# Convolution, Gelu and two matmuls on one core: a new order for the first transfers, diagonals on GpSimd, and taps in two calls

## The chip, the cores and the metric

The kernel runs on one core of a Trainium2 chip. The metric is device time in microseconds (us) per execution. A run of a one-core program has no second core to compare with, so its state is taken from the time alone; every run told here counted as fast. Each run also has a mean granted TensorE clock, 1.0 being full speed.

Two terms recur. The *software ring* is the DMA queue whose transfers GpSimd issues; SyncE and ScalarE issue to hardware queues (q0 software_dynamic, q1 and q10 hardware_dynamic on the page). *Slot* means one piece of work of TensorE and ScalarE: twelve first-layer matmuls and one Gelu of 1.02 us behind them. Blocks 0 to 5 have eight slots each.

## The reference

```python
def attn(x, weight):                      # x: [8, 4096, 192], weight: [8 heads, 7]
    w = softmax(weight, axis=-1)
    # causal, depthwise: each head's 7 weights serve its 24 channels
    return sum(w[h, k] * x_pad[:, s + k, h*24:(h+1)*24] for k in range(7))

def moe(x, w_in, w_out):                  # x: [32768, 192], w_in: [192, 2048], w_out: [2048, 192]
    h = x @ w_in
    g = 0.5 * h * (1.0 + erf(h / sqrt(2)))
    return g @ w_out

out = moe(attn(x, weight).reshape(32768, 192), w_in, w_out)
```

(Written shorter than the original, with the same arithmetic. All inputs and outputs are float32.)

## The kernel before

Blocks of 256 tokens (six of them), then of 512, from two halves of the token range at once. Blocks 0 and 1 are convolved on TensorE with diagonal matrices `dg` made of the tap weights, all later ones on VectorE, tap by tap (ScalarE makes the first tap of three of them). TensorE multiplies by `W_in`, ScalarE applies Gelu, and TensorE multiplies the previous block's result by `W_out` between the slots of the current one. The parts that matter here are all about the start:

```python
# GpSimd: W_in in three parts (256, 256 and 512 columns of each half), cast to bf16 by the DMA
win_in(FP[0], FP[1], S_WIN[0])
...                                        # two affine selects make the identity
for i in range(1, 3):
    win_in(FP[i], FP[i + 1], S_WIN[i])
halo(0); halo(1)                           # cut: block 0 needs shifted copies between rows
for p in range(NP):
    cast(g, 1, p)                          # x of block 1 to bf16
for i in range(4):                         # W_out to bf16, a quarter at a time
    g.wait_ge(S_WOUT[i], 16)
    o = 2 * WG[i] * C
    g.tensor_copy(wout[:, o : o + 4 * C], woutf[:, o : o + 4 * C]).then_inc(S_WOG)

# SyncE: all other loads
load(sp, 0, (0, 1))                        # half of block 0's x; ScalarE issues the other half
sp.wait_ge(S_WIN[0], 32)                   # first part of W_in has landed
load(sp, 1)
for i in range(4):
    sp.dma_start(woutf[...], woutt[...]).then_inc(S_WOUT[i], 16)
load(sp, 2)
load(sp, 3)

# VectorE: one tap of the convolution, three calls (p = 0, 1, 2), blocks 2 and later
ins = v.scalar_tensor_tensor(dst, src, wk, a, op0=ALU.mult, op1=ALU.add)

# TensorE, while block 1's slots run: the second layer of block 0
if n == 1 and un in ((0, 0, 0), (0, 0, 4)):
    t.wait_ge(S_WOG, 2 + un[2] // 2)
```

## Time and profile before

| | before |
|---|---|
| time, median of 4 runs | 682.74 us (682.60 to 683.16) |
| span of the profiled run | 680.6 us |
| mean granted clock | 1.0 |
| first Gelu | 10.10 us |
| first matmul of block 1 | 18.34 us |
| first Gelu of block 2 | 29.73 us |
| x of block 0, of block 1, of block 2 landed | 5.91, 12.75, 19.2 us |
| W_in parts landed | 6.67, 8.69, 10.69 us |
| W_out quarters landed | 13.60, 14.65, 15.71, 17.40 us |

(682.81 us was the median of the three runs known at the time of the prediction.) From 18.34 us on, TensorE works without a gap, so from there only what would hold TensorE up can cost time. Ahead of that, everything waits for data, and all of the weights, plus x of the first three blocks, come through the same sixteen DMA engines in the first 20 us, whose share is 1.13 from 4 to 15 us and 1.25 from 15 to 20 (the windows are below). The prediction shows the lines.

### The profile page before, as it was taken

How to read it: one execution, taken by the hardware profiler on the slowest of the kernel's cores; microseconds unless marked ns; L12 is line 12 of the kernel's file. 1: busy time of each engine (PE TensorE's matmuls, PEld its weight loads, DVE VectorE, ACT ScalarE, POOL GpSimd, SP SyncE). 2: the span in 40 equal slices, each digit the busy share in tenths (PEclk: the TensorE clock that was granted, in tenths of full speed). 3: DMA queues.
4: the chain of work that ended last, by engine and by line, in shares of the span. 5: the costliest groups of instructions: out<-in, count | busy, mean ns of one | idle time of the engine just before them, and what ended most of it. 6: DMA issues, size and time to landing. Idle time of an engine off the chain costs nothing.

```text
span 680.6 us, 27316 instructions
## 1 busy us (share of the span) xinstructions
PE 674.6 (99%) x12576; PEld 407.5 (60%) x12576; DVE 561.7 (83%) x906; ACT 536.5 (79%) x548; POOL 38.9 (6%) x57
## 2 busy tenths in 40 slices
PE   8999999999999999999999999999999999999998
PEld 4999655555555555555555555555555555555557
DVE  6999989888889888899888898888898888988611
ACT  6899987787787877787777788777778777778772
POOL 5126000000000000000000000000000000000000
PEclk9999999999999999999999999999999999999999
DMA  9446233134442133331244422334322444310123
GB/s 223 88 99 138 64 71 81 43 69 95 96 94 61 45 87 94 95 89 46 59 95 94 94 70 45 78 94 96 89 56 47 95 94 96 80 40 25 48 50 94
DMA packets 132994, 54.79 MB, mean 81 GB/s; under 512 B 126480, under 2 KB 132752, under 8 KB 132880
## 3 DMA queue, kind: packets, MB, share of 16 engines
q1 hardware_dynamic: 130960, 51.50, 32.6%
q8 instruction: 98, 1.61, 1.0%
q0 software_dynamic: 1248, 0.79, 0.9%
q10 hardware_dynamic: 672, 0.76, 0.4%
q14 instruction: 16, 0.13, 0.1%
HBM read 28.66 MB, written 25.17 MB: 79 GB/s over the span
## 4 chain that ended last, share of the span: by engine, by line
PE 98%; ACT 1%; DMA 1%; DVE 0%; SPq 0%; issue 0%; ACTq 0%
PE hp L763 48%; PE ob L823 43%; PE ob L793 5%; PE hp L793 1%; DMA xin<-in_x_dram 1%; ACT gT L684 1%; PE ob L714 0%; ACT xc L191 0%; DVE xT L529 0%; ACT xTb L633 0%; SPq L871 0%; DVE osb L283 0%; SPq L332 0%; ACTq L632 0%
## 5 line engine op out<-in xcount | busy, mean ns | idle before, releaser
L684 ACT ACTIVATE gT<-hp 128x1024 bf16<-128x1024 f32 x512 | 523.2, 1024 | 129.0 <-PE hp L763 125.7
L763 PE MATMUL hp<-xc,win 64*64 64x512 bf16 (+2 forms) x6048 | 418.6, 366 | 1.5 <-ACT gT L684 1.1
L823 PE MATMUL ob<-gT,wout 64*64 64x512 bf16 x5376 | 366.3, 376 | 0.0
L562 DVE SCALAR_TENSOR_TENSOR acc<-xT,wcol,acc 128x512 f32<-128x512 f32 (+1 forms) x495 | 314.5, 699 | 0.0
L763 PEld LDWEIGHTS hp<-xc,win 64*64 64x64 bf16 (+1 forms) x6048 | 187.6, 106 | 136.1 <-ACT gT L684 2.6
L823 PEld LDWEIGHTS ob<-gT,wout 64*64 64x64 bf16 x5376 | 172.1, 118 | 123.0
L314 DVE STREAM_TRANSPOSE osb<-ob 128x512 f32<-128x512 f32 x84 | 74.1, 885 | 99.9 <-PE ob L823 99.9
L529 DVE STREAM_TRANSPOSE xT<-xin 128x512 f32<-128x512 f32 (+1 forms) x105 | 78.5, 797 | 3.4 <-DMA xin<-in_x_dram 3.4
L562 DVE SCALAR_TENSOR_TENSOR xc<-xT,wcol,acc 128x512 bf16<-128x512 f32 (+1 forms) x99 | 65.1, 712 | 0.0
L450 POOL COPY xT<-xT 128x18 f32<-128x18 f32 x30 | 27.9, 929 | 505.3 <-DVE xT L529 483.0
L793 PE MATMUL ob<-wout,gT 64*128 64x192 bf16 x896 | 46.8, 243 | 0.0
L793 PEld LDWEIGHTS ob<-wout,gT 64*128 64x128 bf16 x896 | 38.6, 94 | 5.2 <-issue 0.4
L555 DVE TENSOR_SCALAR acc<-xT,wcol 128x512 f32<-128x512 f32 (+1 forms) x90 | 37.5, 473 | 1.1
L698 PE MATMUL hp<-warm 128*128 128x512 bf16 x16 | 5.5, 516 | 1.3 <-DVE warm L466 1.3
L285 ACT ACTIVATE osb<-ob 128x192 f32<-128x192 f32 x2 | 0.7, 331 | 7.1 <-PE ob L793 7.1
L793 PE MATMUL hp<-wout,gT 64*128 64x192 bf16 x128 | 5.9, 243 | 0.0
L283 DVE COPY osb<-ob 128x192 f32<-128x192 f32 x2 | 0.7, 358 | 6.1 <-PE ob L793 6.1
L793 PEld LDWEIGHTS hp<-wout,gT 64*128 64x128 bf16 x128 | 5.3, 94 | 0.0
L657 ACT ACTIVATE acc<-xT,wcol 128x256 f32<-128x256 f32 (+1 forms) x9 | 5.2, 575 | 0.0
L270 ACT ACTIVATE osb<-ob 128x384 f32<-128x384 f32 x10 | 4.9, 486 | 0.0
L698 PEld LDWEIGHTS hp<-warm 128*128 128x128 bf16 x16 | 1.9, 126 | 4.3 <-issue 2.5
L387 POOL DMA_DIRECT2D win<-in_moe_w_in_dram x6 | 3.9, 660 | 0.8 <-POOLq L904 0.8
(36 smaller groups left out, 31.4 us busy)
## 6 DMA issues: line engine op xcount, KB each, us to landing
out_dram<-osb SPq DMA_DIRECT2D x122, 192.0 KB, 3.1
xin<-in_x_dram SPq DMA_DIRECT2D x116, 192.0 KB, 4.1
xin<-in_x_dram SPq DMA_DIRECT2D x20, 96.0 KB, 4.3
woutf<-in_moe_w_out_dram SPq DMA_DIRECT2D x4, 384.0 KB, 5.9
win<-in_moe_w_in_dram POOLq DMA_DIRECT2D x4, 96.0 KB, 4.6
win<-in_moe_w_in_dram POOLq DMA_DIRECT2D x2, 192.0 KB, 5.1
out_dram<-osb SPq DMA_DIRECT2D x8, 48.0 KB, 1.7
out_dram<-osb ACTq DMA_DIRECT2D x4, 96.0 KB, 2.0
```

The lines of the kernel that those rows point to most:

```text
L270: e.activation(out=dst, in_=src, func=AF.Copy).then_inc(S_EVA)
L314: v.transpose(ap(osb[m % 2], j, [[8 * C, 128], [C // 2, TB // 32], [NP, 32]]), bank(ring(m, j)),).then_inc(S_EV)
L450: g.tensor_copy(dst, src).then_inc(S_HALO)
L529: v.transpose(ap(xT[n % 2], p * XW + HX, [[NP * XW, 128], [1, w]]), ap(xin[n % NX], p, [[TB // 32 * DQ, 128], [D if n == 0 else DQ, w // 3 ...
L555: ins = v.tensor_scalar(a, src, wk, None, ALU.mult)
L562: ins = v.scalar_tensor_tensor(dst, src, wk, a, op0=ALU.mult, op1=ALU.add)
L657: a.activation(out=acc[n % 2][:, p * TB : p * TB + w], in_=ap(xT[n % 2], p * XW + HX, [[NP * XW, 128], [1, w]]), func=AF.Copy, scale=wcol[ ...
L684: a.activation(out=ap(gT[n % 2], i * c * 2 * w, dst), in_=ap(hp[u % 2], 0, src), func=AF.Gelu,).then_inc(S_GELU)
L698: t.matmul(hp[1][:, 0:512], warm[:, 0:128], warm[:, :])
L763: ins = t.matmul(hp[u % 2][fo : fo + fw, o : o + w], ap(win, f1, [[NP * F, 64], [2, fw]]), xc[n % 2][r, p * TB : p * TB + w], start=(p == ...
L793: ins = t.matmul(bb[sub], gT[m % 2][r, c0 : c0 + 128], wout[r, CH[sub][i] * C : (CH[sub][i] + 1) * C], start=(ph == 0 and i == 0), stop=(p ...
L823: ins = t.matmul(bank(ring(m, j), slice(64 * h, 64 * h + 64), w), ap(wout, 64 * hf * NF * C + CH[h][i] * C + j, [[NF * C, 64], [NP, 64]],) ...
```

## The change

Its intent: start block 0 and block 1 sooner. The software ring carries half of W_in, then x of block 1, then the other half; so x of block 1 arrives earlier than on SyncE behind W_in. GpSimd makes `dg`, which frees VectorE of 0.63 us (the trace before). x of block 0 comes in half rows of 96 floats and needs no shifted copies. VectorE does a tap in two calls (two thirds, then one), and the three transposes of a block in one.

```diff
 # GpSimd
-            win_in(FP[0], FP[1], S_WIN[0])
             g.wait_ge(S_MSET, 1)
             ...                                   # affine selects
-            for i in range(1, 3):
-                win_in(FP[i], FP[i + 1], S_WIN[i])
+            win_in(FP[0], FP[1], [S_WIN[0]] * 2)
+            load(g, 1, (0, 2), S_XP)
+            g.wait_ge(S_PRO, 9)
+            g.wait_ge(S_IDN, 2)
+            g.tensor_tensor(dg, idb, wcol, ALU.mult).then_inc(S_DG)      # shortened
+            load(g, 1, (1, 3), S_XP)
+            win_in(FP[1], FP[2], S_WIN[1:])
 # SyncE
-            sp.wait_ge(S_WIN[0], 32)
-            load(sp, 1)
-            for i in range(4):
-                sp.dma_start(woutf[...], woutt[...]).then_inc(S_WOUT[i], 16)
-            load(sp, 2)
+            sp.wait_ge(S_WIN[1], 16)
+            for k in range(3):
+                wout_in(k)
+            load(sp, 2)
+            wout_in(3)
             load(sp, 3)
 # SyncE and ScalarE, loads of block 0: as all others now
-                if n == 0:
-                    dst = [[TB // 32 * DQ, 32], [1, mb * D - DQ]]
-                    src = [[mb * D, 32], [1, mb * D - DQ]]
-                else:
-                    dst = ...
+                dst = [[TB // 32 * DQ, 32], [DQ, mb], [1, DQ]]
+                src = [[D, 32], [32 * D, mb], [1, DQ]]
 # VectorE
-            def conv(n, k, p):                     # p in 0, 1, 2
+            def conv(n, k, s):                     # s in 0, 1
+                p0, pn = (0, 2) if s == 0 else (2, 1)
 # TensorE
-            for i in range(16):                    # warm-up
+            for i in range(10):
-            share = {1: [4, 12, 8, 8, 8, 8, 8, 8]}
+            share = {1: [4, 4, 4, 10, 10, 10, 11, 11]}
-                        if n == 1 and un in ((0, 0, 0), (0, 0, 4)):
-                            t.wait_ge(S_WOG, 2 + un[2] // 2)
+                        if n == 1 and un[:2] == (0, 0) and un[2] % 4 == 0:
+                            t.wait_ge(S_WOG, 1 + un[2] // 4)
```

Cut: the order of W_out's chunks to match, the semaphores' counts, the order of TensorE's convolutions and of its first slot, block 0's copies out of the convolution, and the store of block 0. `share` says how many pieces of block 0's second layer TensorE does behind each slot of block 1.

## The prediction

> **What bounds the kernel now.** I read the page first, parts 1, 2 and 4.
>
> ```profile
> PE 674.6 (99%) x12576; PEld 407.5 (60%) x12576; DVE 561.7 (83%) x906; ACT 536.5 (79%) x548; POOL 38.9 (6%) x57
> PE   8999999999999999999999999999999999999998
> PE 98%; ACT 1%; DMA 1%; DVE 0%; SPq 0%; issue 0%; ACTq 0%
> ```
>
> TensorE is busy in 99% of the span, only the first and last slices are below nine tenths, and the chain that ended last is 98% TensorE. So whatever the change does to VectorE over the long middle is hidden, and it can move only the start, some 20 us. I then read the chain in order of time over the first 32 us.
>
> ```profile
> 1.64 4.26 DMA xin<-in_x_dram
> ...
> 7.02 0.97 PE ob L714 x18
> ...
> 9.12 0.28 ACT xc L191
> ...
> 9.45 0.63 PE hp L763 x8
> 10.08 0.02 issue
> 10.10 1.94 ACT gT L684 x2
> 12.04 0.01 issue
> 12.05 1.03 ACT gT L684
> 13.09 0.05 issue
> 13.13 0.83 PE hp L763 x12
> ...
> 17.26 1.03 ACT gT L684
> 18.29 0.04 issue
> 18.34 0.83 PE hp L763 x12
> ```
>
> The chain is: x of block 0 lands at 5.90, is transposed and cast, goes through the convolution on TensorE (L714), is copied out by ScalarE, then meets W_in (L763) and the first Gelu at 10.10. Block 0 has eight slots, each with a Gelu of 1.02 us against 0.66 us of matmul, so ScalarE paces it. Block 1 starts at 18.34, and from there TensorE never waits. What ScalarE lost in between is in the timeline of the start.
>
> ```profile
> 12.77 1.34 DVE L529 STREAM_TRANSPOSE xT<-xin 128x256 f32<-128x256 f32 x3 [1.93 <-DMA xin<-in_x_dram]
> 13.36 1.47 POOL L213 CAST xTb<-xT 128x256 bf16<-128x256 f32 x3 [5.53 <-DVE xT L529]
> 15.98 1.02 ACT L684 ACTIVATE gT<-hp 128x1024 bf16<-128x1024 f32 x1 [0.95 <-PE hp L763]
> 17.26 3.96 ACT L684 ACTIVATE gT<-hp 128x1024 bf16<-128x1024 f32 x4 [0.25 <-PE hp L763]
> 19.24 1.35 DVE L529 STREAM_TRANSPOSE xT<-xin 128x256 f32<-128x256 f32 x3 [0.77 <-DMA xin<-in_x_dram]
> ```
>
> x of block 1 lands only at 12.77; its cast comes late, TensorE stands in front of block 1's convolution, and ScalarE waits 0.95 + 0.25 = 1.20 us. The last line matters for the rivals: x of block 2 lands at 19.24, and VectorE's taps hang on it.
>
> [...]
> - [...] 15 taps of 256 columns take 6.02 us (0.40 each), 15 of 512 take 10.04 us (0.67 each). So a tap is about 0.13 us plus 1.05 ns per column. [...]
> - [...] For the 448 columns of the diagonals [...] VectorE takes 0.63 us here. No line of this trace shows such an operation on GpSimd.
> - [...] New x of block 0 is in rows of 384 B. The part of the page on queues over the first 24 us gives 42 ns per packet on the hardware queue of SP (61.3% of 16 x 24 us, over 5552 packets) and 360 ns per packet of 5760 B on ACT's queue (6.0%, over the 64 data packets).
> - [...] the warm-up's weight loads follow 0.43 us apart until 5.05, and then six take 1.18 us. The new kernel has 10 warm-up matmuls, not 16.
>
> **The change part by part.**
> 1. *x of block 0 in half rows.* Old: four loads of 180 KB, each row read twice; 128 packets x 360 ns / 16 engines = 2.9 us of the engines. New: four of 96 KB in 384-byte rows; 1024 packets x 42 ns / 16 = 2.7 us, at the 27 ns that the whole run's average gives (32.6% of the span over 130960 packets) 1.7 us. W_in's first half is issued after the two affine selects, about 0.5 us later than its first quarter was, so it crowds x less. I choose a landing 0.5 us sooner, at 5.4 (between 0 and 0.9). The shifted copies on GpSimd (three of 0.39 us) go, but they ran beside ScalarE's casts and ended with them (7.68 against 7.72), so that alone is worth nothing.
> 2. *Diagonals on GpSimd.* The tap weights are there at 4.6 as before. GpSimd has by then issued two parts of W_in and two of x, four issues of 0.65 us from about 1.9, until 4.6. [...] The convolution can start at 5.4 + 0.05 + 0.54 + 0.47 = 6.5, where it was 7.02. [...]
> 3. *Copying out of block 0.* ScalarE had four copies (0.38, 0.38, 0.28, 0.28) and now has three, VectorE has the fifth piece. The last one moves forward by 0.30 us. The first slot now does both chunks' first two thirds before it needs the last third: four matmuls (0.27 us) remain after that copy instead of eight (0.63). I count 0.45 us of the possible 0.6, since the first eight matmuls must also be done.
> 4. *First Gelu:* 10.10 - 0.5 - 0.45 = 9.15.
> 5. *The duplication of W_in* is now in halves: two copies of 0.98 us from 8.5 to 10.5, and the third slot needs them; it could start at 10.15. Its matmul of 0.66 to 0.83 us then ends 0.1 to 0.25 after the second Gelu: a loss of 0.15.
> 6. *x of block 1 on the software ring*, issued at about 3.3 to 4.6 and 5.7 to 7.0, lands near 9.5 by the ring's 4.6 us from issue. Transposes run from 10.5, GpSimd's casts of 0.49 each end near 12.5, in time for its convolution behind slots 3 to 5. So the 1.20 us of ScalarE's waits go.
> 7. *Second half of W_in*, issued at 7.1 to 8.4, lands at 12 to 13; slot 4 wants it at 12.3. A loss of 0 to 0.5 us; I count 0.2.
> 8. *W_out* is issued only when that has landed, at about 12.1 where it was 8.5. Landed at 15 to 17, cast in pieces of 0.88 us. The first second-layer matmuls come near 17.1 and take four units in each of the first three slots, in the order in which the pieces land. I count 0.1 us there, with nearly no slack.
> 9. *Taps in two calls.* In a block of 256 a tap of three calls is 3 x 0.40 = 1.20 us; now 0.67 + 0.40 = 1.07. Over six such taps 0.8, the first tap (0.29 per 256, 0.41 per 512 columns) 0.18 and the joined transposes 0.2 make 1.1 us per block. In blocks of 512: 0.13 x 6 + 0.1 + 0.2, about 1.1 us in each of the 29, which takes some 33 us from VectorE's 561.7 (to near 529). None of it is on the path in the middle, but it is needed in blocks 2 and 3: there the taps ended at 28.62 and 39.17, while TensorE started these blocks at about 28.79 and 39.3. An earlier TensorE without faster taps would have run into VectorE.
>
> Sum: 0.5 + 0.45 + 1.20 - 0.15 - 0.2 - 0.1 = 1.7 us at the start of block 1. Block 1's first three slots become paced by ScalarE (1.03 against 0.99 us of TensorE work), another 0.1; I leave 0.2 more for what block 2 may cost. So 1.4 us of 682.81: 681.4 us.
>
> **The rivals.**
> - *The wait moves to x of block 2.* Its loads are behind three parts of W_out that wait for W_in. If they land at 19.7 rather than before 19, the taps (1.15 + 0.70 + 6 x 1.07 = 8.27 us) end at 28.0, and block 2 cannot start much before 27.6, where 27.3 is wanted. For it: DMA is saturated until 20 now. Against: 336 KB less is moved, and VectorE's chain is shorter by 1.1 us. The gain would be 0.9 to 1.1 us: 681.8.
> - *GpSimd becomes the bound of the start.* If its issues or the diagonals take half as long again, [...] all that follows on its ring shifts by 1 us: W_in's second half lands at 13.5, and ScalarE waits a microsecond at slot 4. Against: the six issues were steady at 0.62 to 0.78 us. Gain about 0.3: 682.5.
> - *A cold TensorE.* The warm-up now ends near 5.3 and leaves a gap before 6.5. [...] the convolution (1.69 us) and the first slots run up to twice as long: 1 to 2 us lost, 683. Against: in the trace the clock was full from 5.05.
> - *All goes well* and x lands at 5.0, nothing stalls: 2.1 us gained, 680.7.
>
> **Range and chances.** The whole start up to 18.34 holds only some 9 us of waits and ramp, most of it the fixed chain of landing, transpose, convolution, Gelu; 2% would be 13.7 us. A gain beyond 2% would need the middle to move, and TensorE has no gap there; a loss beyond 2% would need VectorE to fall behind by a third of a microsecond in each block, and it becomes faster. So within 2% is nearly certain. The four cases give 680.7 to 683; I take 680.6 to 682.6 around 681.4.
>
> **What would show it.** Right: the first transpose at about 5.4; the first Gelu near 9.2; no ScalarE wait of 0.9 us between slots 5 and 6; block 1's first matmul near 16.6; VectorE busy near 529 us with TensorE's busy time unchanged but for the warm-up; no wait of TensorE for VectorE at block 2. Wrong: a tensor_tensor line of GpSimd well over 1.2 us, or ending after 6.5; a transposition of block 2 that waits for DMA past 19.5; W_in waits in front of slot 4; matmuls of 0.43 us after 6 us; or waits of TensorE past 40 us, which would mean that the taps or evacuations in the middle were on the path after all.

## The result, and the profile after

The changed kernel took 686.78 us (median of 4 runs, 686.50 to 687.35). The ratio to before is 1.0058, 95% interval 1.0043 to 1.0072. Ratios here and below are the mean time of one kernel's fast runs over that of the other's of the same rounds, so not quite the ratio of the medians quoted. The change is within 2%, as predicted, but 0.6% slower where 0.2% faster was predicted, and outside the predicted range.

First the busy times and the chain that ended last, from the page of the changed kernel:

```profile
PE 676.2 (99%) x12570; PEld 410.1 (60%) x12570; DVE 527.3 (77%) x610; ACT 536.0 (78%) x547; POOL 31.5 (5%) x56
PE 96%; DMA 2%; SPq 1%; POOL 0%; DVE 0%; issue 0%; ACT 0%; ACTq 0%
```

VectorE became 34 us lighter, as predicted, but it has 0% of the chain in either kernel, so this by itself shortened nothing. DMA went from 1% to 2% of the chain and SyncE's sequencer appears with 1%; before, TensorE had 98%. So the start has become longer. From the first Gelu of block 4 to the end, the profiled runs of both kernels and of nearly all experiments take 629.78 to 629.83 us (one with three-call taps 630.07). All that follows is about the first 35 us.

The chain of waits of the changed kernel, in order of time (start, length, what):

```profile
6.73 4.22 DMA win<-in_moe_w_in_dram
...
10.96 0.40 SPq L853
...
15.68 7.44 DMA woutf<-in_moe_w_out_dram
...
23.18 0.96 POOL wout L431
```

Before, this stretch of the chain was matmuls and Gelus. Now it goes through the second half of W_in, which SyncE waits for before it issues W_out (L853). The last quarter of W_out is issued at 15.68, behind x of block 2, and takes 7.44 us; GpSimd then casts it, and TensorE goes on at 24.19. The timeline of the same stretch (start, busy time, engine, what, count, and in brackets the idle time before and who ended it) shows what that did to the engines:

```profile
5.76 2.37 PE L682 MATMUL ob<-xTb,dg 64*64 64x256 bf16 x56
9.19 3.89 ACT L652 ACTIVATE gT<-hp 128x1024 bf16<-128x1024 f32 x4 [0.73 <-PE hp L740]
16.95 0.83 PE L740 MATMUL hp<-xc,win 64*128 64x256 bf16 x12 [0.45 <-ACT gT L652]
19.29 0.50 PE L771 MATMUL ob<-wout,gT 64*128 64x192 bf16 x8 [0.52 <-POOL wout L431]
20.93 0.50 PE L771 MATMUL ob<-wout,gT 64*128 64x192 bf16 x8 [0.49 <-POOL wout L431]
24.19 2.03 PE L771 MATMUL ob<-wout,gT 64*128 64x192 bf16 x20 [2.10 <-POOL wout L431]
27.54 1.02 ACT L652 ACTIVATE gT<-hp 128x1024 bf16<-128x1024 f32 x1 [4.38 <-PE hp L740]
```

The first Gelu came at 9.19 (predicted 9.15) and block 1's first matmul at 16.95 (predicted near 16.6; before 18.34). Up to there the change gained 1.39 us. Then TensorE waited three times for a quarter of W_out, 0.52 + 0.49 + 2.10 = 3.1 us, and ScalarE had nothing to do for 4.38 us.

The trace also shows, by the sixteen updates of each transfer's semaphore, when each of the sixteen DMA engines finished its part of a quarter. The second quarter was complete on fifteen of them at 16.66 and on the last at 18.35; the third at 18.24 and 20.00; the fourth was complete on fourteen at 21.32 and on all at 23.13. With a cast of 0.83 us, the second and third would have been ready before TensorE came for them (at 18.77 and 20.44). So the waits of 0.52 and 0.49 us are those of one late engine. Without any such lag about 1.2 us of the 3.1 would have been left, at the fourth quarter (an estimate from these times). In the repeat of this kernel below, the first two waits were absent and the third was 2.9 us.

What the same work cost in each kernel is in the windows from block 1's first matmul to block 2's first Gelu: one stretch of the kernel before, then three of the changed one, split at 24.15 and 27.56 (columns: stretch, length, busy time and count of PE, PEld, DVE, ACT, POOL, granted clock, DMA share, GB/s).

```profile
18.34:29.73 11.39, 11.39 (x242) 10.71 (x244) 10.58 (x28) 9.59 (x11) 0.40 (x2) 1.00 0.37 72
```

```profile
16.95:24.15 7.20, 4.13 (x72) 3.09 (x72) 2.40 (x3) 4.92 (x5) 2.62 (x4) 1.00 0.99 209
24.15:27.56 3.41, 3.31 (x36) 2.52 (x38) 3.41 (x8) 0.02 (x1) 0.18 (x1) 0.50 0.06 13
27.56:33.96 6.40, 6.33 (x138) 5.81 (x136) 6.37 (x12) 4.84 (x7) 0.45 (x1) 1.00 0.10 33
```

Before: 11.39 us without a gap. After: 17.01 us, of which TensorE was idle 3.07 + 0.10 + 0.07 = 3.24. Its busy time grew by 13.77 - 11.39 = 2.38. The middle stretch explains most of that: the clock stood at 0.50 for 3.41 us, so half of its 3.31 busy us, 1.66, is slowness. The remaining 0.72 is for the greater part a cost of the new `share`. TensorE's weight loads waited twice for TensorE's own last matmul (total, times, longest), first in this kernel, then in the run with the transfers' order undone:

```profile
PEld ob L771 <- PE ob L771: 0.7, 2, 0.4
```

```profile
PEld ob L769 <- PE ob L769: 0.6, 2, 0.3
```

Block 0's second layer has 64 pieces, and the program makes the piece after the 16th and the one after the 48th wait until the pieces before it are done. With the old shares (4, 16, ... 40, 48 pieces done after a slot) both points lay between two slots, with first-layer matmuls in between; with the new ones (4, 8, 12, 22, 32, 42, 53) they lie inside the fourth and the seventh slot. The kernel before has no such wait. Its size can be read where nothing else held TensorE up after block 1's first matmul: in five of the runs below (W_out issued earlier, W_out after x of block 1, transfers' order undone, the same with taps in three, block 1 held back) it is 11.87 us from block 1's first matmul to block 2's first Gelu, against 11.39 before and 11.40 with the new taps alone. So 0.48 us go with the new shares, whatever the transfers do; no run changed the shares alone. About 0.24 stays unassigned. The account is +3.24 (waits) + 1.66 (half clock) + 0.48 (shares) + 0.24 (unassigned) - 1.39 (earlier start) = +4.23 us at block 2's first Gelu, 33.96 against 29.73; the spans differ by 684.8 - 680.6 = 4.2.

Why was W_out late? The DMA engines' windows, before and then after. The share is the time of all packets over that of sixteen engines; packets overlap, so it can pass 1.

```profile
4.00:15.00 11.00, 9.57 (x155) 5.71 (x152) 7.01 (x18) 7.66 (x14) 4.82 (x12) 1.00 1.13 247
15.00:20.00 5.00, 4.59 (x104) 3.43 (x100) 4.04 (x9) 3.78 (x5) 3.31 (x5) 1.00 1.25 238
20.00:24.00 4.00, 4.00 (x92) 3.82 (x88) 3.96 (x12) 3.09 (x4) 0.32 (x1) 1.00 0.30 57
```

```profile
4.00:15.00 11.00, 10.21 (x189) 6.80 (x186) 7.77 (x18) 7.82 (x14) 5.96 (x12) 1.00 0.82 159
15.00:20.00 5.00, 4.03 (x80) 3.11 (x74) 1.03 (x4) 4.57 (x5) 1.26 (x2) 1.00 1.10 275
20.00:24.00 4.00, 1.60 (x30) 0.99 (x24) 2.25 (x3) 2.05 (x2) 1.65 (x2) 1.00 0.87 184
```

Before keeps the engines full until 20 us. The changed order leaves them at 0.82 between 4 and 15 us, moving 159 x 11 = 1749 KB where before moved 247 x 11 = 2717 KB (150 KB of the difference is the end of block 0's x, which before read 336 KB more in all). The difference is (1.13 - 0.82) x 11 = 3.4 us of the engines' time. Of this 0.6 is that x, by its packets, and 0.3 is W_in that the changed kernel had moved before 4 us. The other 2.5 us have to be made up later: from 20 to 24 us the engines still run at 0.87, where before they were nearly done (0.30). In the run with the transfers' order undone the share from 4 to 15 us was 0.99. W_out's quarters landed at 14.55, 18.35, 20.0 and 23.13 us, x of block 2 at 21.69.

| | before | after |
|---|---|---|
| x of block 0 / block 1 / block 2 landed | 5.91 / 12.75 / 19.2 | 4.29 / 9.39 / 21.69 |
| W_in last part landed | 10.69 | 10.95 and 12.01 |
| W_out issued | 8.54 to 10.13 | 10.96 to 15.68 |
| W_out last quarter landed | 17.40 | 23.13 |
| clock first full | 5.01 | 7.08 |
| mean clock of the four runs | 1.0 | 0.998, 0.998, 0.995, 0.995 |

One half-clock stretch of 3.41 us makes 3.41 x 0.5 / 684.8 = 0.25% of the mean clock. By that estimate, two runs had one such stretch and two had two; only the profiled one has a trace.

### The profile page after: what moved, and what is told of

It is laid out like the page before. It is cut to its first block, busy times and chain, and to the rows that moved or that the text cites. A ratio compares the mean times of both kernels' runs of the same rounds, so it can differ in the third digit from the quotient of the medians.

```text
span 684.8 us, 26995 instructions
## 1 busy us (share of the span) xinstructions
PE 676.2 (99%) x12570; PEld 410.1 (60%) x12570; DVE 527.3 (77%) x610; ACT 536.0 (78%) x547; POOL 31.5 (5%) x56
## 4 chain that ended last, share of the span: by engine, by line
PE 96%; DMA 2%; SPq 1%; POOL 0%; DVE 0%; issue 0%; ACT 0%; ACTq 0%
PE hp L740 47%; PE ob L801 42%; PE ob L771 5%; DMA woutf<-in_moe_w_out_dram 1%; PE hp L771 1%; DMA win<-in_moe_w_in_dram 1%; SPq L853 0%; SPq L339 0%; DMA wsb<-in_weight_dram 0%; POOL xin L339 0%; POOL wout L431 0%; POOL dg L397 0%; DVE wcol L460 0%; ACT wex L593 0%; DVE osb L295 0%
## 5 line engine op out<-in xcount | busy, mean ns | idle before, releaser
L536 DVE SCALAR_TENSOR_TENSOR acc<-xT,wcol,acc 128x1024 f32<-128x1024 f32 (+1 forms) x330 | 296.1, 952 | 4.9 <-ACT acc L625 4.9
L508 DVE STREAM_TRANSPOSE xT<-xin 128x1536 f32<-128x1536 f32 (+2 forms) x39 | 74.2, 1909 | 5.7 <-DMA xin<-in_x_dram 5.6
L536 DVE SCALAR_TENSOR_TENSOR xc<-xT,wcol,acc 128x1024 bf16<-128x1024 f32 (+1 forms) x66 | 60.5, 956 | 0.0
L421 POOL COPY xT<-xT 128x18 f32<-128x18 f32 x30 | 19.6, 654 | 511.3 <-DVE xT L508 483.5
L529 DVE TENSOR_SCALAR acc<-xT,wcol 128x512 f32<-128x512 f32 (+2 forms) x60 | 34.3, 613 | 1.1
L202 DVE CAST xc<-ob 64x256 bf16<-64x256 f32 (+3 forms) x8 | 2.9, 357 | 3.1 <-PE ob L682 2.9
L682 PEld LDWEIGHTS ob<-xTb,dg 64*64 64x64 bf16 x112 | 3.3, 117 | 1.6 <-ACT xTb L225 0.9
```

Source lines behind the costliest of these rows:

```text
L421: g.tensor_copy(dst, src).then_inc(S_HALO)
L508: v.transpose(out, src).then_inc(S_TR)
L529: ins = v.tensor_scalar(a, src, wk, None, ALU.mult)
```

## The experiments

The theories at the outset. *W*: W_out is late because of its place in the issue order, behind the wait for W_in and, for the last quarter, behind x of block 2; another place mends it. *D*, the rival: the DMA engines are the bound of the start, and whatever is moved ahead pushes something else back. *C*: the half clock is the larger part of the loss. Edits are to the changed kernel unless said otherwise. Each call's kernels ran on one chip together with the kernel before; its medians there were 682.71, 683.38, 682.62 and 682.93 us.

All results, with the first Gelu of block 2 as the trace of the profiled run has it (before 29.73, after 33.96):

| run | median us | ratio to before, 95% | block 2's first Gelu |
|---|---|---|---|
| W_out issued earlier | 685.35 | 1.0045 (1.0028 to 1.0061) | 31.89 |
| W_out ahead of x of block 2 | 683.97 | 1.0015 (1.0000 to 1.0030) | 30.00 |
| TensorE kept warm | 683.80 | 1.0015 (1.0000 to 1.0030) | 31.07 |
| both W_out edits | 685.06 | 1.0029 (1.0010 to 1.0048) | 30.27 |
| W_out after x of block 1 | 683.17 | 0.9993 (0.9979 to 1.0006) | 31.75 |
| before, W_out late | 684.11 | 1.0010 (0.9996 to 1.0023) | 31.82 |
| diagonals on VectorE | 682.59 | 0.9989 (0.9968 to 1.0011) | 31.77 |
| before, new taps | 682.59 | 0.9987 (0.9974 to 1.0001) | 30.29 |
| the changed kernel again | 685.83 | 1.0043 (1.0026 to 1.0061) | 33.31 |
| transfers' order undone | 683.07 | 1.0005 (0.9992 to 1.0019) | 30.97 |
| ring alone undone | 684.04 | 1.0017 (1.0003 to 1.0030) | 31.53 |
| order undone, taps in three | 683.21 | 1.0009 (0.9995 to 1.0023) | 30.18 |
| order undone, block 1 held back | 684.90 | 1.0031 (1.0013 to 1.0049) | 31.11 |
| half of W_out's bytes | 681.82 | 0.9986 (0.9973 to 0.9999) | 29.22 |

### W_out issued earlier

```diff
-            sp.wait_ge(S_WIN[1], 16)
+            sp.wait_ge(S_WIN[0], 32)
```

> The changed kernel with one edit: SyncE issues W_out as soon as the first half of W_in has landed (8.2 us), not the first part of the second half (10.95). Theory W (the loss is W_out's late landing: TensorE waits 3.1 us for its casts in block 1, then runs 3.4 us at half clock): pieces 1 to 3 land about 2.7 us sooner, the first two waits go, and the fourth piece, still behind x of block 2, lands near 20.5 instead of 23.1; TensorE waits at most 0.5 us, the clock stays full, and the time is 681.3 to 682.3. Rival D (DMA throughput is the limit, so an earlier W_out only pushes W_in's second half and x of block 1 back): ScalarE waits before slot 4 of block 0 instead and the time stays above 684.

TensorE's waits in its first 60 us no longer show W_out at all. They show this (total, times, longest):

```profile
PE hp L740 <- DMA win<-in_moe_w_in_dram: 3.0, 1, 3.0
```

The second half of W_in landed at 12.91 and 15.32 instead of 10.95 and 12.01, while three quarters of W_out, issued from 7.59 to 8.55, shared the engines with it. The wait was exchanged for one of the same length (0.9 us of it is the lag of the last of sixteen engines, 14.43 to 15.32). The profiled run was the fastest; the other three had a mean clock of 0.997 or 0.998. This is D's outcome and W's miss. The transfers are issued by different engines (W_in by GpSimd, W_out by SyncE), and still the one delayed the other, here by 2 to 3.3 us.

### W_out ahead of x of block 2

```diff
-            for k in range(3):
+            for k in range(4):
                 wout_in(k)
             load(sp, 2)
-            wout_in(3)
```

> The changed kernel with one edit: all four pieces of W_out are issued before x of block 2; the wait for the second half of W_in stays. Theory W: the fourth piece lands near 20.5, so the longest wait (2.1 us) shrinks under 0.5 and the half clock with it; but x of block 2 lands 1 to 1.5 us later than its 21.7, its taps end about 32, and TensorE, which would be at block 2 at 29 to 30, waits there for VectorE for 2 to 3 us. Time 683.5 to 685.5. If only the fourth piece mattered: 682.5 or less. If the loss were elsewhere: 686.8 unchanged.

683.97 us, as W expected. The last quarter of W_out landed at 19.31, no wait of TensorE for W_out is listed any more, and no run showed a clock under 0.999. x of block 2 landed at 20.88, sooner than the 21.69 before the edit and not later, but not early enough for VectorE's taps:

```profile
PE hp L740 <- DVE xc L536: 1.2, 1, 1.2
```

So most of the loss goes with this one line: 683.97 - 682.71 = 1.3 us of it is left. What is left is a new wait at block 2 and the shares' 0.48 us. The profile flatters the edit: this run was the fastest, its clock happened to be first full at 4.26 rather than 7.08, and its first Gelu came at 8.49 rather than 9.19. It is the wait that the prediction's first rival had named.

### TensorE kept warm

```diff
+                            if un[2] == 12:
+                                for _ in range(9):
+                                    t.matmul(bank(3), warm[:, 0:128], warm[:, :])
                             t.wait_ge(S_WOG, 1 + un[2] // 4)
```

> The changed kernel with nine matmuls of zeros into a free PSUM bank while TensorE waits for the fourth piece of W_out. If the half clock from 24.1 to 27.6 is a loss of its own that follows from the idle time, it goes and the time falls by 1.7 to 2.0 us to about 685.0. If the half clock is only a mark of waiting that would happen anyway, nothing changes (686.8).

The windows of this kernel just after its wait for W_out, where the changed kernel's clock fell to half (granted clock third from the end):

```profile
24.00:26.00 2.00, 2.00 (x46) 1.88 (x42) 2.00 (x5) 1.02 (x1) 0.00 (x0) 1.00 0.03 9
```

The clock was 1.0 in all runs and the time fell by 3.0 us, more than the 1.7 to 2.0 expected (by 2.0 us, if the repeat of the changed kernel below, 685.83, is taken for it; this call had no changed kernel of its own). Of this, W_out's last quarter happened to land 1.3 us sooner in the profiled run (21.80 rather than 23.13), and by the estimate above two of the changed kernel's four runs had had two half-clock stretches. So C's mechanism is shown, and a size of about 1.7 us for one stretch fits. But in the account above the half clock is the smaller part (1.66 us against 3.24 of waits), and it is a consequence: it followed TensorE's wait for W_out.

### Both W_out edits together

The two edits above in one kernel.

> Both edits of the first two runs: W_out whole, issued at 8.2 us, before x of block 2. Theory W: W_out lands by about 17.5 and x of block 2 by about 19.3, as in the kernel before; no wait of TensorE for W_out, the start of block 1 stays at 16.9, block 2 waits at most 0.5 us for its taps, and the time is 681.2 to 681.8, 1.0 to 1.5 us under the kernel before. Rival D: W_in's second half lands later than 13 and the time is 683 or more.

A miss: 685.06, and not under 682. In the profiled run (682.87, the fastest) W_in's second half landed at 11.95 and 13.56, and TensorE waited 1.3 us for it. A landing later than 13 and a median over 683 are both of D's signs. The other three runs, without a trace, had a mean clock of 0.998, which is what one half-clock stretch makes by the estimate above. From here I held W to be half of the story at most.

### W_out behind x of block 1

```diff
-            sp.wait_ge(S_WIN[1], 16)
-            for k in range(3):
+            sp.wait_ge(S_XP, 64)
+            for k in range(4):
                 wout_in(k)
             load(sp, 2)
-            wout_in(3)
```

> The changed kernel with SyncE's W_out issued when x of block 1 has landed (about 9.0 us, between the 7.7 of the run with both edits and the 10.9 of the changed kernel), all four pieces before x of block 2. Theory E (what matters is that the 16 DMA engines stand partly idle from about 11 to 15 us while everything still to land waits; W_in's second half must finish first and W_out must be queued right behind it): W_in's second half still lands by 11.5 to 12.5, W_out's fourth piece at 17.5 to 18.5, x of block 2 by 19.5; TensorE waits under 0.4 us for each; time 681.3 to 682.5. Rival V (landings jitter by over a microsecond from run to run, and any order without slack loses): 683.5 or more with a wait for W_in or for the taps in the profile.

683.17 us, ratio 0.9993: equal to before. The profiled run was its slowest (684.35). There, one DMA engine of sixteen completed the last part of W_in at 13.68, the other fifteen by 12.0. TensorE waited 1.7 us for it, and the clock was at half from 14.76 to 18.17. Between the theories; on the time it decides nothing.

### Before, with W_out issued late

An edit to the kernel before: `sp.wait_ge(S_WIN[2], 32)` ahead of the four W_out transfers, so that they are issued at 11.1 instead of 8.5.

> The kernel before with one wait added: SyncE issues W_out only when the last part of W_in has landed (10.7 us where it was 8.5). Theory W alone, in the other kernel: W_out and x of block 2 land about 2 us later, VectorE's taps of block 2 end 2 us later (30.8, TensorE wants them at 28.8) and the time rises by 1.5 to 2.5 us to 684.2 to 685.2. If a late W_out were harmless where the rest is as before: 682.7 unchanged.

W_out landed at 19.50, x of block 2 at 21.41. TensorE waited 1.5 us for VectorE's taps and 0.3 for W_out; block 2's first Gelu came 2.1 us later than in the kernel before. So in this trace late W_out and late x of block 2 hold that kernel up too, without any of the rest of the change. In time it is not shown: only 0.7 us (1.0010, the interval holds 1): short of the 1.5 to 2.5 expected, where the kernel before itself varied (682.55 to 684.47).

### Diagonals on VectorE again

The reordered W_out (as above), and `dg` made by VectorE, so that GpSimd's ring doesn't pause for it.

> The run with the order edit (W_out whole before x of block 2, still behind W_in), with the diagonals back on VectorE, so that GpSimd issues the rest of its ring without a pause. Second half of W_in issued from 4.5 instead of 6.7 us and landed about 1 us sooner (9.8 and 10.9), so W_out and x of block 2 about 1 us sooner (18.3 and 19.9); against that the transposes of block 0 start 0.65 us later behind the diagonals. Theory E: time 682.5 to 683.5, below the 684.0 of the order edit. If the pause of the ring is worth nothing: 684.0 to 684.6.

The second half of W_in was issued 1.1 us sooner (5.58 and 6.20) and landed at 10.93 and 12.10: not sooner at all. The expected mechanism missed. So in this trace the pause of the ring cost no landing. The convolution started at 6.24, where with the diagonals on GpSimd it was 5.75. The runs fell apart into two at 681.2 to 681.3 and two at 683.9 to 684.4; the median, inside the expected range, lies in the gap between them and confirms nothing. The two fast ones have no trace.

### The new taps alone

The kernel before with taps in two calls and joined transposes.

> The kernel before with one part of the change alone: taps in two calls and joined transposes from block 2 on. VectorE busy falls by some 33 us; TensorE has no gap that ends on VectorE, so the time stays at 682.4 to 682.9. [...]

```profile
PE 674.2 (99%) x12576; PEld 407.4 (60%) x12576; DVE 529.3 (78%) x612; ACT 536.6 (79%) x548; POOL 33.5 (5%) x57
```

VectorE's 561.7 us became 529.3 and the time 682.59, ratio 0.9987 with an interval up to 1.0001. As expected, this part is off the path. It seems to give slack: in this run x of block 2 came as late as 20.44, and TensorE didn't wait for VectorE; but block 1 also started 0.55 us later than in the kernel before.

### The changed kernel again

> The changed kernel once more, as the control of this call on its chip. Every theory: 686 to 687.5, the start of block 2's first Gelu near 34 us, a wait of TensorE for the W_out casts of over 2 us, and a clock record that falls to half in it.

685.83 us, with runs from 683.76 (clock 1.0) to 687.47 (0.997). In the profiled one TensorE waited 2.9 us once for W_out's casts, and the clock was at half from 23.86 to 27.27. The median is just under the expected 686, and one run shows no half clock. So the loss repeats, but its size varies by 3.7 us between runs.

### The transfers' order undone, all else kept

```diff
 # GpSimd: both halves of W_in back to back
             win_in(FP[0], FP[1], [S_WIN[0]] * 2)
-            load(g, 1, (0, 2), S_XP)
+            win_in(FP[1], FP[2], S_WIN[1:])
             ...
-            load(g, 1, (1, 3), S_XP)
-            win_in(FP[1], FP[2], S_WIN[1:])
 # SyncE
             load(sp, 0, (0, 1))
+            load(sp, 1, sm=S_XP)
-            sp.wait_ge(S_WIN[1], 16)
-            for k in range(3):
+            sp.wait_ge(S_WIN[0], 32)
+            for k in range(4):
                 wout_in(k)
             load(sp, 2)
-            wout_in(3)
```

> The changed kernel with its order of transfers undone: both halves of W_in follow each other on the software ring, x of block 1 goes on SyncE's hardware ring directly behind x of block 0, and all of W_out behind it as soon as W_in's first half has landed, before x of block 2. Theory E (16 DMA engines have about 16 us of work before block 2; the changed order leaves them partly idle between 4 and 15 us): two rings work from 2 us on, W_in's second half lands by 10.5 to 11.5, W_out's last piece by 17.5, x of block 2 by 19; TensorE waits nowhere over 0.4 us; time 1.0 to 1.8 us under the kernel before of the same rounds (ratio 0.9975 to 0.9985). If the landings are slow whatever the order: ratio above 1.000 with a wait for W_out or x.

I had expected 0.9975 to 0.9985; it was 1.0005. There was no wait for W_out, and the clock was 1.0 throughout. But x of block 1 now travelled beside the first half of W_in, which landed at 9.82 instead of 8.19:

```profile
PE hp L738 <- DMA win<-in_moe_w_in_dram: 2.5, 1, 2.5
```

The 2.8 us that the changed kernel lost against this one (685.83 - 683.07) are the transfers' order. The gain that should then have been left was eaten by W_in: block 1's first matmul came at 19.10, 0.76 us later than before, and with the shares' 0.48 that is the 1.24 us by which block 2's first Gelu was late (30.97 against 29.73). This is where W fell for good.

### The ring alone undone

The W_in halves back to back and x of block 1 on SyncE, while SyncE's wait for W_in and x of block 2 ahead of W_out's last quarter stay.

> Only the ring undone: as the run before it in this call, but SyncE still holds W_out back until the second half of W_in lands (10 us) and still puts x of block 2 before W_out's fourth piece. Theory E: W_out starts about 1 us sooner than in the changed kernel, its fourth piece lands near 21 to 22, TensorE waits 0.5 to 1.5 us for it; ratio 1.001 to 1.003 where the changed kernel has 1.006. If the ring's order is harmless in itself: no different from the control.

1.0017, the ratio as expected, but the mechanism only in part. W_out was issued at 10.64, hardly sooner. TensorE waited 1.3 us for W_out's last quarter (landed 22.26), as expected, and also 1.8 us for W_in, which I had not in mind.

### Order undone, and taps in three calls

> The second run of this call with VectorE's taps in three calls again. If the two calls are needed once TensorE starts earlier: the taps of block 2 end about 1 us later, TensorE waits 0.5 to 1.2 us for VectorE at block 2 and perhaps at block 3, and the time is that much above the second run. If not needed: the same time within 0.3 us.

1.0009; no wait of TensorE for VectorE is to be seen. Block 1 started as late here as in the kernel before, so this doesn't test whether the faster taps are needed after an earlier start. It shows only that they are not needed without one.

### Order undone, x of block 1 held back until the first half of W_in has landed

An edit to the run with the transfers' order undone:

```diff
             load(sp, 0, (0, 1))
+            sp.wait_ge(S_WIN[0], 32)
             load(sp, 1, sm=S_XP)
```

> The changed kernel with the order of transfers of the kernel before, in halves: both halves of W_in back to back on the software ring; SyncE waits for W_in's first half (7.3 to 8.2 us), then issues x of block 1, all of W_out, x of block 2. The runs so far say that the DMA engines have a fixed amount of work before block 2 and that each order only chooses what waits. If an order exists that keeps both the early first Gelu and the early W_out, it is this one: first Gelu 9.0 to 9.3, x of block 1 landed by 11.5, a wait of 0.3 to 0.8 us for its cast, W_out whole by 17.5, x of block 2 by 19.5; ratio 0.997 to 0.999. If the trade is fixed: x of block 1 or W_in lands later than 12, TensorE waits over 1 us there, ratio 0.9995 to 1.002.

One of the waits of TensorE:

```profile
PE ob L680 <- POOL xTb L227: 1.0, 1, 1.0
```

The first matmul of the first layer came sooner (9.13 against 9.95), but x of block 1 later (12.78), and TensorE waited 1.0 us for its cast (the line) and still 1.6 us for W_in: 1.0031. It looks like a trade again, but 1.3 us of the wait for W_in is one late engine: all other parts of the first half had landed by 7.73, the last at 9.00. And the six runs are of two kinds: three at 683.07 to 683.67 with a clock of 1.0, three at 686.12 to 686.82 with 0.997 or 0.998. So this run does not show that the order itself makes the trade.

### Half of W_out's bytes

The changed kernel with its own order, but each W_out transfer brings only half of its columns, and the cast reads them twice. The result is wrong; the instructions of the compute engines have the same number and size.

```diff
-                    ap(woutf, 2 * k * C, [[NF * C, 128], [8 * C, 2], [1, 2 * C]]),
+                    ap(woutf, 2 * k * C, [[NF * C, 128], [8 * C, 2], [1, C]]),
```

(and the source likewise.)

> The changed kernel, its order untouched, with half the bytes of W_out (each row of two chunks loads the first alone and the cast uses it twice: a wrong result on purpose). If the throughput of the DMA engines behind the late start is the cause: W_out takes 2.8 us of the engines instead of 5.6, its fourth piece lands near 20.5 and x of block 2 near 19.5, the waits of TensorE for W_out fall under 0.7 us, no half clock, time 680.8 to 682.3 (ratio 0.997 to 0.9995). If a fixed latency or the wait of SyncE alone were the cause, and bytes did not matter: the fourth piece still at 22 to 23 and the time above 685.

```profile
PE ob L772 <- POOL wout L432: 0.3, 1, 0.3
```

W_out's quarters landed at 14.15, 15.24, 15.89 and 19.96, x of block 2 at 18.18, and there was no half-clock stretch. 681.82 us, 0.9986 (0.9973 to 0.9999). With fewer bytes the very order that lost 4 us gains about 1. So it is the bytes that have to pass the engines that make the order fail. That the rest of the change brings 1 us is not shown: the interval only just leaves out 1, and the kernel before was not run with half of W_out's bytes, which could have helped its x of block 1.

## Why the prediction was wrong

The size of the effect was within 2%, as said. The sign and the range were wrong.

- *Step 1, x of block 0:* predicted at 5.4, landed at 4.29. Its 384-byte packets took 23 ns each, not the 42 ns that I took from the queue's average, which mixed in larger packets. The gain of 1.1 us more was given back: the convolution ran until 8.12, in 2.37 us rather than 1.69, since the clock was full only from 7.08; and the first half of W_in landed at 8.19.
- *Step 2, diagonals:* 0.94 us on GpSimd, done at 5.62. When the prediction was made no trace had shown their time there; the issue times from 5.7 on in steps 6 and 7 rest on the author's assumption of it. The convolution, predicted for 6.5, started at 5.76, since x came sooner: 0.14 us after the diagonals, and the chain that ended last goes through them (0.94 us). With the diagonals on VectorE it started at 6.24; what that is worth in time no run shows.
- *Steps 3 and 4, first Gelu:* 9.19 against 9.15. Right in the sum by luck: x came 1.1 us sooner than written, and the slow convolution gave it back.
- *Step 5, duplication of W_in:* 0.69 us per copy rather than 0.98, which was the mean of two copies in the trace before, of 0.69 and 1.28. Harmless.
- *Step 6, x of block 1:* 9.39 against "near 9.5". Right, and it made block 1 start at 16.95.
- *Step 7, W_in's second half:* 10.95 and 12.01, at or ahead of the early end of "12 to 13". Right.
- *Step 8, W_out: the step that failed.* "Landed at 15 to 17 ... I count 0.1 us there, with nearly no slack." It landed at 14.55 to 23.13; in its place stand 3.24 us of TensorE's idle time and 1.66 of half clock behind it. I had given each transfer a latency, as if it had the engines to itself. And the fourth quarter, which stands behind x of block 2 in SyncE's queue, wasn't issued before 15.68 and then took 7.44 us, where the median of the kernel before was 5.9. The sum was there to be made: by the traces' packet times x of block 0, W_in, x of block 1, W_out and x of block 2 want about 1.5 + 5.7 + 1.3 + 5.6 + 1.9 = 16 us of all sixteen engines (an estimate from packet counts and mean durations). Before starts at 2 us and ends at 19.2. An order that is 2.5 us of the engines' time short by 15 us ends near 19.2 + 2.5 = 21.7. It ended at 23.1, with fourteen engines done at 21.3.
- *The shares:* the prediction left 0.1 us for block 1's first slots and 0.2 "for what block 2 may cost". The new shares cost 0.48 us in block 1, for a reason that it did not name: TensorE waiting for its own last matmul.
- *Step 9, taps:* VectorE 527.3 us against "near 529". Right, and off the path, as the taps alone showed.
- *The rivals.* The first had the right place (DMA behind W_out) but x of block 2 as the victim; in the changed kernel it was W_out's last quarter, issued behind that x. The reordered kernels then showed the predicted wait for x of block 2, 1.2 us. The cold-TensorE rival considered the beginning alone. The clock did come late there, but with the same ten warm-up matmuls it was first full anywhere from 3.95 to 7.17 us in the other runs; its costly fall was at 24 us, after a wait.

Why did mending the order gain nothing that could be measured? W_in, x of block 1, W_out and x of block 2 share the sixteen engines, whose share is 0.98 to 1.25 from 2 to 20 us in the kernel before. Undoing the wait for W_in delayed W_in by up to 3.3 us; moving x of block 1 delayed W_in by 1.6 us; putting W_out first left x of block 2 at 20.9. Each is in a trace. Two more terms add to this. The shares take 0.48 us in every one of these orders. And where the clock fell, far more was lost: of the fourteen runs of "W_out issued earlier", "both W_out edits" and "block 1 held back", the nine with a mean clock of 0.997 or 0.998 took 684.88 to 686.82 us, the five with 1.0 took 682.87 to 684.47. None of the kernels that move all bytes beat before: the best ratios, 0.9987 to 0.9993, have intervals that hold 1. Only the one with fewer bytes is below.

What stays open: whether some order keeps the 1.4 us in every run, as single runs at 681.2 did; whether the new transfers would gain with the old shares; why one DMA engine of the sixteen now and then completes up to 2.5 us behind the others; why one of SyncE's W_out issues took 0.6 to 2.2 us in eight of the profiles (0.47 in another; in all eight it overlapped a packet of 16 KB on the DMA queue that the profile lists as "instruction", which is a coincidence in time and was not tested); and 0.24 us of TensorE's busy time.

## What to carry to other kernels

When a start is bound by loads, add up the bytes, or better the packets' times, of everything that must have landed by then, and compare that with the engines' share in the windows. In the kernel before the share was at its top (1.13 from 4 to 15 us, 1.25 from 15 to 20). Here reordering exchanged one wait for another (with W_out issued earlier, 3.0 us for W_in in place of 3.1 us for W_out), and the order that made a transfer wait for another's landing left engines idle that were missed later (0.82 instead of 1.13 from 4 to 15 us, 2.5 us of the engines' time to be made up). A wait of TensorE of two microseconds can be dearer than it is: after one of 2.10 us the clock's fall cost another 1.7 here. And when work is shared out anew over the slots, look where its own inner waits come to lie (0.48 us here).

## What the traces show of packets, landings and the clock

- Rows of 384 B of block 0's x took 23 ns each, 16.7 bytes per ns on one engine; the packets of 1536 B of W_out, on busier engines, took 79 ns on average before and 87 after, 18 to 19. So the loss against longer rows was small here.
- The sixteen engines' completions of one transfer lay apart: W_out's second quarter had fifteen by 16.7 us and the last at 18.4; in the kernel before all sixteen of each quarter came within 1.2 to 1.7 us.
- The clock fell to 0.50 after a gap of TensorE of 2.10 us, with two shorter ones (0.52 and 0.49) before it: in the 3.22 us from 20.93 to the fall at 24.15, TensorE worked for 1.16. Another run (W_out after x of block 1) fell after a gap of 1.72 us, while gaps of 2.96 (W_out issued earlier) and 2.45 (order undone) brought no fall: in these runs the length of the gap alone doesn't decide. The stretch at half clock was 3.41 us in the changed kernel (24.15 to 27.56), in its repeat (23.86 to 27.27) and in the run with W_out after x of block 1 (14.76 to 18.17).
- Over the fifteen traces that record it (all but that of the new taps alone) the clock was first full between 3.95 and 7.17 us, with the first matmul always at 1.26: a spread of 3.2 us.
